# Queueing a group's output scaling behind the next fill's first two evacuations

## Chip, cores, metric

The kernel runs on one core of a Trainium2 chip. The metric is device time of one execution in microseconds (us). Times of single steps and instructions come from one profiled run of each kernel.

Engines are named as in the profile: PE (TensorE matmuls), PEld (its weight loads), DVE (VectorE), ACT (ScalarE), POOL (GpSimd).

## The reference

For each of 4 batches, 32 inducing rows attend to 12480 tokens, the tokens then attend to the 32 results, and every token goes through a two-layer network with a per-channel leaky ReLU.

```python
h   = mab(inducing, x)            # 32 x 128 per batch: softmax attention over 12480 tokens
y   = mab(x, h)                   # 12480 x 128: softmax attention over 32 rows
hid = y @ w_in                    # 128 -> 2048
g   = maximum(hid, 0) + alpha * minimum(hid, 0)
out = g @ w_out                   # 2048 -> 128
```

The leaky ReLU is split as `alpha*hid + (1-alpha)*relu(hid)`. So the output is a sum of two parts: a ReLU part through all 2048 channels, and a *linear term*, which is one small 128x128 product. Both are computed on unnormalised attention weights, and the output is divided by the softmax denominator at the very end. That division is the *output scaling*.

## The kernel before

The tokens are cut in groups of 512, 25 groups to a batch. A group takes four *steps*, j = 0 to 3. One step is a fill (four matmuls into four PSUM banks), four evacuations with ReLU by ACT or DVE, and one step later 16 output matmuls into an accumulator.

The kernel uses eight banks of PSUM, the memory that its matmuls write. Six form a ring for the fills and for side work. The two others are accumulators that groups use in turn.

```python
def fill(st, g, j):
    # four matmuls into the next four banks of the ring (K=32, 512 columns each)
    for r in range(4):
        mm(bank(), hW[32*r:32*r+32, j, :], rep[32*r:32*r+32, :w])     # cut
    if j == 2:
        linear(st, lin_groups(st.b, g))
    for r, (ps, i) in enumerate(banks):
        # a small clock model picks the engine that would be done first
        if ta <= td: nc.scalar.activation(out=gt[:, r, :w], in_=ps, func=RELU)
        else:        nc.vector.tensor_relu(gt[:, r, :w], ps)

def mm2(st, g, j, gt, done):
    acc = accs[(st.b * NG + g) % 2]
    # 16 matmuls: acc += gt.T @ W1                                      # cut
    if j == NJ - 1 and st.b * NG + g > 0:
        finish(st, g)          # DVE: ob = acc * 1/denominator, then the store

def lin_groups(b, g):          # even g: for g and for g + 1
    ...
def linear(st, groups):
    for k in range(NB):
        for r, g in enumerate(groups):
            mm(accs[(st.b*NG + g) % 2][:pp, k, :], rep..., hA...,
               start=(r == 1 and k == 0))   # starts the accumulator of g + 1

# main loop: the output matmuls of a step stand behind the fill of the next
for b, g, j in fills:
    gt, done = fill(states[b], g, j)
    for fn in tasks.pop((b * NG + g, j), []): fn()
    if prev is not None: mm2(*prev)
    prev = (states[b], g, j, gt, done)
```

The ring is short. Four banks of a fill plus four of the next are eight, but there are six, so a fill's third and fourth banks are the first and second banks of the fill before. Those two must be evacuated within one step.

The scaling of group g-1 is emitted after the evacuations of fill (g, 0), so DVE meets it at about fill (g, 1). The linear term in (g, 2), g even, starts the accumulator of group g+1, which is the one that group g-1 has just used, so it must wait until that scaling has read it.

`a_scores` and `a_accum` work on the next batch and stood in j=1, of odd and of even groups. `b_scores` and `b_den` stand in j=3 of even groups. Each takes one bank of the ring and some PE time.

The softmax here doesn't subtract the row's maximum and nothing guards it: scores larger than these inputs give would overflow.

Of the kernel before, what the change touches and what calls it, by code (L numbers as in the profile page):

```python
# [15 lines left out]
P = 128  # L16
# [8 lines left out]
def kernel(  # L25
# [64 lines left out]
    clk = {"P": 0.0, "A": 0.0, "D": 0.0}  # L90
    free = [0.0] * RING

    def bank():
        i = ring_n[0] % RING
        ring_n[0] += 1
        clk["P"] = max(clk["P"], free[i])
        return ring[i]

    def spent(e, ns, release=True):
        clk[e] = max(clk[e], clk["P"] + 100) + ns  # L100
        if release:
            free[(ring_n[0] - 1) % RING] = clk[e] + 100

    def mm(o, lhsT, rhs, start=True, stop=True, **kw):
        return pin(nc.tensor.matmul(o, lhsT, rhs, start=start, stop=stop, **kw))  # L105
# [163 lines left out]
    def h_sum(st):  # L269
        st.et = work.tile([P, 1], f32, name="et", tag="et")  # L270
        pin(nc.vector.reduce_sum(out=st.et[:], in_=st.es[:], axis=AXX))

    def h_den(st):
        ps = bank()
        mm(ps[:, 0:1], fold[:], st.et[:])
        rh = work.tile([P, 1], f32, name="rh", tag="rh")
        pin(nc.vector.reciprocal(out=rh[:], in_=ps[:, 0:1]))
        st.fr = work.tile([P, P], f32, name="fr", tag="fr")
        pin(nc.vector.tensor_scalar_mul(out=st.fr[:], in0=fold[:], scalar1=rh[:]))


    def h_transpose(st):
        ps = bank()
        mm(ps[:, :P], st.hacc[:], st.fr[:])
        st.hT4 = work.tile([C, P], bf16, name="hT4", tag="hT4")
        pin(nc.vector.tensor_copy(out=st.hT4[:], in_=ps[:, :P]))
        st.hT = st.hT4[:, 0:M]

    def h_weights(st):
        ps = bank()  # L290
        for r in range(4):
            mm(
                ps[32 * r : 32 * r + 32, :], st.hT,
                w_in_b[:, r * NJ * P : (r + 1) * NJ * P],
            )
        st.hW = work.tile([P, NJ, P], bf16, name="hW", tag="hW")
        pin(nc.vector.tensor_copy(out=st.hW[:].rearrange("m j k -> m (j k)"), in_=ps[:]))

    def h_linear(st):
        pa = bank()  # L300
        mm(pa[:, :C], st.hT4[:], Amat[:])
        st.hA = work.tile([P, C], bf16, name="hA", tag="hA")
        pin(nc.vector.tensor_copy(out=st.hA[:], in_=pa[:, :C]))
# [52 lines left out]
    def b_den(st, s):  # L356
        e2 = st.e2.pop(s)
        ps = bank()
        clk["P"] += 240
        spent("D", 250)  # L360
        if s < NS:
            for j in range(NB):
                mm(ps[:, j * NQ : (j + 1) * NQ], e2[:, j * P : (j + 1) * P], pick[:])
            rd = work.tile([P, NB, NQ], f32, name="rd", tag="rd")
            pin(nc.vector.reciprocal(
                out=rd[:].rearrange("p j q -> p (j q)"), in_=ps[:, : NB * NQ]
            ))
        else:
            for j in range(JR):
                mm(ps[:PR, j : j + 1], e2[:, j * PR : (j + 1) * PR], pick[0:M, 0:1])  # L370
            rd = work.tile([PR, JR, 1], f32, name="rdr", tag="rdr")
            pin(nc.vector.reciprocal(
                out=rd[:].rearrange("p j q -> p (j q)"), in_=ps[:PR, :JR]
            ))
        st.rden[s] = rd


    def shape_of(g):
        return (P, NB) if g < NS * NQ else (PR, JR)

    def fill(st, g, j):
        pp, nb = shape_of(g)
        w = pp * nb
        rep = st.rep[g]
        gt = gt_pool.tile([P, 4, GRP], bf16, name="gt", tag="gt")
        banks = []
        for r in range(4):
            ps = bank()
            mm(
                ps[:, :w], st.hW[32 * r : 32 * r + 32, j, :], rep[32 * r : 32 * r + 32, :w]  # L390
            )
            banks.append((ps, (ring_n[0] - 1) % RING))
        if j == 2:
            linear(st, lin_groups(st.b, g))
        ca, cd = w * 0.75 + 96, w * 1.04 + 68
        ready = clk["P"] + 150 + w * 0.42
        clk["P"] = ready - 50 + (240 if j == 2 and lin_groups(st.b, g) else 0)
        done = ready
        for r, (ps, i) in enumerate(banks):
            ta, td = max(clk["A"], ready) + ca, max(clk["D"], ready) + cd  # L400
            if ta <= td:
                clk["A"] = free[i] = ta
                pin(nc.scalar.activation(out=gt[:, r, :w], in_=ps[:, :w], func=RELU))  # L403
            else:
                clk["D"] = free[i] = td
                pin(nc.vector.tensor_relu(gt[:, r, :w], ps[:, :w]))  # L406
            free[i] += 150
            done = max(done, free[i])
        return gt, done

    def mm2(st, g, j, gt, done):
        pp, nb = shape_of(g)
        acc = accs[(st.b * NG + g) % 2]
        clk["P"] = max(clk["P"], done) + 4 * nb * 57
        begun = g % 2 == 1 and st.b + g > 1
        for r in range(4):
            c = r * NJ + j
            for k in range(nb):
                mm(
                    acc[:pp, k, :], gt[:, r, k * pp : (k + 1) * pp], W1[:, c, :],  # L420
                    start=(j == 0 and r == 0 and k == 0 and not begun), stop=False,
                    skip_group_check=True,
                )
        if j == NJ - 1 and st.b * NG + g > 0:
            finish(st, g)



# [1 line left out]
    def lin_groups(b, g):  # L430
        if g % 2 == 0 and (b, g) != (0, 0):
            return [g, g + 1] if g + 1 < NS * NQ else [g]
        return []
# [13 lines left out]
    def finish(st, g):  # L447
        pp, nb = shape_of(g)
        acc = accs[(st.b * NG + g) % 2]
        s, q = divmod(g, NQ)  # L450
        rd = st.rden[s]
        rq = rd[:, :, q : q + 1]
        rbc = bass.AP(tensor=rq.tensor, offset=rq.offset, ap=[rq.ap[0], rq.ap[1], [0, C]])
        ob = ob_pool.tile([P, NB, C], f32, name="ob", tag="ob")
        pin(nc.vector.tensor_tensor(  # L455
            out=ob[:pp, :nb, :], in0=acc[:pp, :nb, :], in1=rbc, op=MULT
        ))
        spent("D", nb * C * 1.04 + 68, release=False)
        t0 = st.b * N + g * GRP
        last_one = (st.b, g) == (B - 1, NG - 1)  # L460
        pin((nc.sync if last_one else nc.gpsimd).dma_start(  # L461
            out=out[t0 : t0 + pp * nb, :].rearrange("(p j) c -> p j c", j=nb),
            in_=ob[:pp, :nb, :],
        ))
        st.rep.pop(g)
# [4 lines left out]
    st = new_batch(0)  # L470
# [90 lines left out]
    n = len(order)  # L561
# [27 lines left out]
    states = {0: st}  # L589
    tasks = {}  # L590

    def at(slot, fn, j=1):
        tasks.setdefault((slot, j), []).append(fn)
# [15 lines left out]
    for b in range(B):  # L609
        base = b * NG  # L610
        for s in range(1, NS + 1):
            g = base + s * NQ - 4
            at(g, lambda b=b, s=s: b_scores(states[b], s), 3)
            at(g + 1, lambda b=b, s=s: b_rep(states[b], s), 3)
            at(g + 2, lambda b=b, s=s: b_den(states[b], s), 3)
        if b + 1 < B:
            n = b + 1

            def begin(n=n):
                states[n] = new_batch(n)  # L620

            at(base, begin)
            for i, u in enumerate(order):
                k = base + i * (NG - 13) // NS
                at(k, lambda n=n, u=u: a_load(states[n], u))
                at(k + 3, lambda n=n, u=u: a_xpose(states[n], u))
                at(k + 5, lambda n=n, u=u: a_scores(states[n], u))
                at(k + 8, lambda n=n, u=u: a_accum(states[n], u))
            k = base + NG - 5
            at(k, lambda n=n: h_sum(states[n]))  # L630
            at(k, lambda n=n: h_den(states[n]), 3)
            at(k + 1, lambda n=n: h_transpose(states[n]))
            at(k + 1, lambda n=n: h_weights(states[n]), 3)
            at(k + 2, lambda n=n: b_scores(states[n], 0))
            at(k + 2, lambda n=n: h_linear(states[n]), 3)
            at(k + 3, lambda n=n: b_rep(states[n], 0), 0)
            at(k + 3, lambda n=n: b_den(states[n], 0))

    prev = None
    for b, g, j in fills:  # L640
        gt, done = fill(states[b], g, j)
        for fn in tasks.pop((b * NG + g, j), []):
            fn()
        if prev is not None:
            mm2(*prev)
        prev = (states[b], g, j, gt, done)
    mm2(*prev)
    assert not tasks, tasks


# [28 lines left out]
```

## Time and profile before

| | before |
|---|---|
| median time | 617.5 us |
| PE busy | 97% of the span |
| DVE busy, ACT busy | 85%, 81% |
| a step in which nothing waits | 1.326 us (400 steps in all) |

These are the page's busy times, and its chain of work that ended last by engine:

```profile
span 615.2 us, 21846 instructions
...
PE 598.9 (97%) x9180; PEld 436.7 (71%) x9180; DVE 524.2 (85%) x935; ACT 500.8 (81%) x994; POOL 89.0 (14%) x151
...
PE 95%; DVE 0%; ACT 0%; issue 0%
```

PE looks full, but that is not the whole truth. In these records a fill matmul lasts 0.38 us and an output matmul 0.22 us, while output matmuls start every 0.056 us and those of a fill within 0.01 us of each other. So a wait of up to 0.3 us disappears under the tail of the matmul before it. The list of waits of PE: its entries are all start-up waits. The only one on the evacuation of a fill is this, and it too is of the first fills (at 30.55 us):

```profile
PE ring_81 L105 <- ACT gt L403: 0.4, 1, 0.4
```

I therefore read *start-to-start* times: a step's length is the time from its first fill matmul to the next step's. Its excess over the shortest step of the same make-up (the same tasks in it) seen in any of the profiles is its stall. The steps before group 2 of the first batch and the last step are left out. Summed by parity of g and by j, in us, the kernel before has:

| slot | even j=0 | even j=1 | even j=2 | even j=3 | odd j=0 | odd j=1 | odd j=2 | odd j=3 | sum |
|---|---|---|---|---|---|---|---|---|---|
| before | 0.1 | 1.5 | 1.8 | 1.8 | 4.5 | 0.4 | 5.9 | 2.9 | 18.8 |

By this measure about 19 of 617 us were waits. The start-up (the first 43 us) is not counted, and a wait that even the shortest step contains would not show. Here is a stall in the timeline, in steps (g, 1) and (g, 2) of an even group. The columns are start, length, engine, line, operation, output and inputs:

```profile
346.50 0.38 PE L105 MATMUL ring_82<-rep,hW 32*128 32x512 bf16 x1
346.51 0.39 PE L105 MATMUL ring_83<-rep,hW 32*128 32x512 bf16 x1
...
346.90 0.68 DVE L455 TENSOR_TENSOR ob<-acc_88,rd 128x512 f32<-128x512 f32 x1
346.98 0.60 ACT L403 ACTIVATE gt<-ring_82 128x512 bf16<-128x512 f32 x1 [0.24 <-ACT gt L403]
347.47 0.59 ACT L403 ACTIVATE gt<-ring_83 128x512 bf16<-128x512 f32 x1
347.50 0.68 DVE L406 TENSOR_SCALAR gt<-ring_84 128x512 bf16<-128x512 f32 x1
347.83 0.10 PEld L105 LDWEIGHTS <-hW 32*128 32x128 bf16 x4
...
347.84 0.38 PE L105 MATMUL ring_82<-rep,hW 32*128 32x512 bf16 x1
...
348.11 0.37 PE L105 MATMUL ring_83<-rep,hW 32*128 32x512 bf16 x1
...
348.12 0.22 PE L105 MATMUL acc_88<-hA,rep 32*128 32x128 bf16 x1
```

The scaling (`ob<-acc_88`) takes DVE at 0.39 us after the fill. ACT then has to evacuate both ring_82 and ring_83, and is done with the second at 348.06. The next fill's last matmul needs ring_83 and starts at 348.11 instead of 347.84. The linear term (`hA`) follows at once. The PE entry carries no idle time, although 0.27 us were lost between two matmuls. In this slot little of it counts: without the wait the linear term would have started 0.23 us after the fill anyway, so the step takes 1.613 us where the shortest of its make-up takes 1.542. In odd groups there is no linear term at j=2, and almost all of such a wait counts (1.583 us against 1.326).

### The profile page before, as it was taken

The page shows a single profiled execution, that of the slowest core. Times are in us where ns is not written, and L with a number is a line of the kernel's source. Part 1 is how long each engine was busy: PE and PEld are TensorE (multiplying, and loading weights), DVE is VectorE, ACT ScalarE, POOL GpSimd, SP SyncE. Part 2 cuts the span into 40 slices and gives each one's busy share as a digit, 9 for nine tenths or more (in the row PEclk, how much of TensorE's full clock was granted, in tenths as well). Part 3 has the DMA queues.
Part 4 walks back from the last instruction along what each step waited for, and adds up shares of the span by engine and source line. Part 5 has one row for each costly group of instructions (what it writes and reads, how often), then busy time and mean ns, then how long its engine had stood idle before and what let it go on. Part 6 is the DMA issues. An engine that isn't in the chain of part 4 may idle for free.

```text
span 615.2 us, 21846 instructions
## 1 busy us (share of the span) xinstructions
PE 598.9 (97%) x9180; PEld 436.7 (71%) x9180; DVE 524.2 (85%) x935; ACT 500.8 (81%) x994; POOL 89.0 (14%) x151
## 2 busy tenths in 40 slices
PE   5799999999999999999999999999999999999996
PEld 4577777777777777777777777777777777777774
DVE  4688888889988888888988888888898888888885
ACT  2678888888888888888878888888888888888884
POOL 7241112101011111111011112110101011011010
PEclk9999999999999999999999999999999999999999
DMA  9824879652125598763122588864121221221211
GB/s 141 173 69 99 185 154 180 152 113 86 51 84 129 125 177 184 144 151 87 58 96 91 111 169 168 171 154 122 62 81 54 86 95 53 80 96 46 87 56 43
DMA packets 87458, 68.66 MB, mean 112 GB/s; under 512 B 53200, under 2 KB 80736, under 8 KB 87360
## 3 DMA queue, kind: packets, MB, share of 16 engines
q0 software_dynamic: 21456, 39.82, 26.2%
q1 hardware_dynamic: 65904, 27.45, 20.4%
q8 instruction: 72, 1.18, 0.8%
q14 instruction: 26, 0.21, 0.1%
HBM read 39.94 MB, written 28.62 MB: 111 GB/s over the span
## 4 chain that ended last, share of the span: by engine, by line
PE 95%; DVE 0%; ACT 0%; issue 0%
PE acc_87 L105 32%; PE acc_88 L105 32%; PE ring_82 L105 5%; PE ring_86 L105 5%; PE ring_84 L105 5%; PE ring_83 L105 5%; PE ring_81 L105 5%; PE ring_85 L105 5%; DVE gt L406 0%; ACT rep L342 0%; ACT gt L403 0%; PE ring_83 L543 0%; PE ring_81 L543 0%; DVE e1T L194 0%; DVE ob L455 0%
## 5 line engine op out<-in xcount | busy, mean ns | idle before, releaser
L105 PEld LDWEIGHTS <-gt 128*128 128x128 bf16 x6272 | 352.9, 98 | 83.0 <-issue 73.6
L105 PE MATMUL acc_87<-W_169,gt 128*128 128x128 bf16 (+1 forms) x3136 | 209.8, 220 | 0.0
L105 PE MATMUL acc_88<-W_169,gt 128*128 128x128 bf16 (+1 forms) x3136 | 209.6, 220 | 0.0
L461 POOL DMA_DIRECT2D out_dram<-ob x99 | 53.6, 541 | 501.6 <-DVE ob L455 482.2
L403 ACT ACTIVATE gt<-ring_86 128x512 bf16<-128x512 f32 (+1 forms) x159 | 92.2, 580 | 17.3 <-ACT gt L403 9.8
L403 ACT ACTIVATE gt<-ring_82 128x512 bf16<-128x512 f32 (+1 forms) x164 | 95.6, 583 | 12.2 <-ACT gt L403 7.9
L403 ACT ACTIVATE gt<-ring_84 128x512 bf16<-128x512 f32 (+1 forms) x151 | 88.5, 586 | 20.0 <-ACT gt L403 15.0
L105 PE MATMUL ring_84<-rep,hW 32*128 32x512 bf16 (+1 forms) x273 | 103.5, 379 | 0.0
L105 PE MATMUL ring_83<-rep,hW 32*128 32x512 bf16 (+1 forms) x273 | 103.0, 377 | 0.0
L105 PE MATMUL ring_81<-rep,hW 32*128 32x512 bf16 (+1 forms) x270 | 102.0, 378 | 0.7 <-ACT gt L403 0.4
L406 DVE TENSOR_SCALAR gt<-ring_81 128x512 bf16<-128x512 f32 (+1 forms) x139 | 91.3, 657 | 13.2 <-PE ring_83 L105 4.8
L105 PE MATMUL ring_86<-rep,hW 32*128 32x512 bf16 (+1 forms) x269 | 101.4, 377 | 0.1
L403 ACT ACTIVATE gt<-ring_85 128x512 bf16<-128x512 f32 x149 | 89.3, 599 | 12.3 <-ACT gt L403 8.4
L105 PE MATMUL ring_82<-rep,hW 32*128 32x512 bf16 (+1 forms) x258 | 97.4, 378 | 0.0
L105 PE MATMUL ring_85<-rep,hW 32*128 32x512 bf16 (+1 forms) x257 | 97.2, 378 | 0.0
L406 DVE TENSOR_SCALAR gt<-ring_83 128x512 bf16<-128x512 f32 (+1 forms) x128 | 84.3, 659 | 12.9 <-PE ring_85 L105 6.0
L406 DVE TENSOR_SCALAR gt<-ring_84 128x512 bf16<-128x512 f32 x122 | 83.6, 685 | 13.5 <-PE ring_86 L105 5.3
L403 ACT ACTIVATE gt<-ring_83 128x512 bf16<-128x512 f32 (+1 forms) x145 | 86.8, 598 | 10.3 <-ACT gt L403 7.5
L403 ACT ACTIVATE gt<-ring_81 128x512 bf16<-128x512 f32 x131 | 78.9, 602 | 19.4 <-ACT gt L403 13.0
L406 DVE TENSOR_SCALAR gt<-ring_85 128x512 bf16<-128x512 f32 (+1 forms) x108 | 72.1, 667 | 12.5 <-issue 5.4
L406 DVE TENSOR_SCALAR gt<-ring_86 128x512 bf16<-128x512 f32 x110 | 75.2, 684 | 7.4 <-ACT gt L403 3.0
L406 DVE TENSOR_SCALAR gt<-ring_82 128x512 bf16<-128x512 f32 x94 | 64.5, 687 | 10.1 <-issue 3.4
(299 smaller groups left out, 377.9 us busy)
## 6 DMA issues: line engine op xcount, KB each, us to landing
out_dram<-ob POOLq DMA_DIRECT2D x96, 256.0 KB, 2.6
rep<-e2d SPq DMA_DIRECT2D x92, 128.0 KB, 3.3
xn<-in_x_dram POOLq DMA_DIRECT2D x18, 512.0 KB, 6.0
xn<-in_x_dram POOLq DMA_DIRECT2D x12, 256.0 KB, 7.7
w_out_f<-in_moe_w_out_dram POOLq DMA_DIRECT2D x1, 1024.0 KB, 13.5
w_in_b<-in_moe_w_in_dram POOLq DMA_DIRECT2D x1, 512.0 KB, 11.4
xT<-xn SPq DMA_TRANSPOSE x18, 4.7
out_dram<-ob POOLq DMA_DIRECT2D x3, 96.0 KB, 2.0
```

What stands on the lines that cost most here:

```text
L105: return pin(nc.tensor.matmul(o, lhsT, rhs, start=start, stop=stop, **kw))
L403: pin(nc.scalar.activation(out=gt[:, r, :w], in_=ps[:, :w], func=RELU))
L406: pin(nc.vector.tensor_relu(gt[:, r, :w], ps[:, :w]))
L461: pin((nc.sync if last_one else nc.gpsimd).dma_start(out=out[t0 : t0 + pp * nb, :].rearrange("(p j) c -> p j c", j=nb), in_=ob[:pp, :nb, :],))
```

## The change

The change evacuates the two banks that the next fill needs first, and scales the finished group after that. The clock model, which picks ACT or DVE for each evacuation, gets other latencies, and two side tasks leave j=1. The core of the diff:

```diff
@@ fill
-        ready = clk["P"] + 150 + w * 0.42
-        clk["P"] = ready - 50 + (240 if j == 2 and lin_groups(st.b, g) else 0)
+        ready = clk["P"] + 240 + w * 0.42
+        clk["P"] = ready - 135 + (240 if j == 2 and lin_groups(st.b, g) else 0)
         for r, (ps, i) in enumerate(banks):
+            if r == 2:
+                while held:
+                    finish(*held.pop())
@@ mm2
-        clk["P"] = max(clk["P"], done) + 4 * nb * 57
+        t = clk["P"]
+        for r in range(4):
+            t = max(t, done[r]) + nb * 57
+        clk["P"] = t + 85
         if j == NJ - 1 and st.b * NG + g > 0:
-            finish(st, g)
+            held.append((st, g))
@@ tasks of the next batch
-                at(k + 5, lambda n=n, u=u: a_scores(states[n], u))
-                at(k + 8, lambda n=n, u=u: a_accum(states[n], u))
+                at(k + 5, lambda n=n, u=u: a_scores(states[n], u), 0)
+                at(k + 8, lambda n=n, u=u: a_accum(states[n], u), 2)
 # cut: held = [] and a list of done times in fill; clock-model lines in h_den, h_transpose, h_weights, h_linear, b_den;
 # one last finish() after the loop
```

More of the change, by code (lines that the diff above doesn't have):

```diff
@@ L274, in h_den @@
         ps = bank()
+        clk["P"] += 250
+        spent("D", 500)
         mm(ps[:, 0:1], fold[:], st.et[:])
@@ L283, in h_transpose @@
         ps = bank()
+        clk["P"] += 300
+        spent("D", 250)
         mm(ps[:, :P], st.hacc[:], st.fr[:])
@@ L290, in h_weights @@
         ps = bank()
+        clk["P"] += 320
+        spent("D", 600)
         for r in range(4):
@@ L300, in h_linear @@
         pa = bank()
+        clk["P"] += 80
+        spent("D", 250)
         mm(pa[:, :C], st.hT4[:], Amat[:])
@@ L358, in b_den @@
         ps = bank()
-        clk["P"] += 240
+        clk["P"] += 130
         spent("D", 250)
@@ L379, in shape_of @@
         return (P, NB) if g < NS * NQ else (PR, JR)
+    held = []
     def fill(st, g, j):
@@ L395, in fill @@
         ca, cd = w * 0.75 + 96, w * 1.04 + 68
-        ready = clk["P"] + 150 + w * 0.42
-        clk["P"] = ready - 50 + (240 if j == 2 and lin_groups(st.b, g) else 0)
-        done = ready
+        ready = clk["P"] + 240 + w * 0.42
+        clk["P"] = ready - 135 + (240 if j == 2 and lin_groups(st.b, g) else 0)
+        done = []
         for r, (ps, i) in enumerate(banks):
+            if r == 2:
+                while held:
+                    finish(*held.pop())
             ta, td = max(clk["A"], ready) + ca, max(clk["D"], ready) + cd
@@ L407, in fill @@
             free[i] += 150
-            done = max(done, free[i])
+            done.append(free[i])
         return gt, done
@@ L647 @@
     mm2(*prev)
+    finish(*held.pop())
     assert not tasks, tasks
```

## The prediction

> **What bounds the kernel now.** TensorE (PE): busy 97% in the page's engine table, 95% of the chain that ended last. The Trainium skill ("Trainium Kernel Development and Optimization", Performance Expectations) warns that matmul busy time is a poor metric because matmuls are pipelined; this trace agrees, for stalls hide inside it. So I read start-to-start times in the timeline. A step (4 fill matmuls, 16 output matmuls) takes 1.326 us when nothing waits. Fill to first output matmul is always 0.317 us, output to next fill always 0.152 us: neither ever waits. What waits are the later fill matmuls, for a bank. Summing each kind of step over its shortest example (g = group, j = step of it) gives: odd g j=2 5.9 us, odd g j=3 2.9, odd g j=0 4.4, even g j=2 1.3, the rest about 1. So about 15 of 617 us can be recovered at all.
>
> **Mechanism before.** VectorE (DVE) scales the finished group (0.68 us) from 0.39 to 1.07 us after the fill of j=1 starts, ahead of its evacuation. ACT then evacuates the first two banks one after the other, the second ends at 1.56, and the next fill (at 1.326) gets its last bank 0.27 us late.
>
> **What changes.** The instruction order shows the same matmuls and evacuation counts (DVE 701, ACT 899), none added. In 98 of 100 groups the j=1 fill is now evacuated ACT, DVE, ACT, ACT, and the scaling sits behind that DVE evacuation. a_scores moves from j=1 to j=0 (0.33 us of PE, no net change), a_accum from j=1 to j=2 (0.34 us, likewise).
>
> Gain: the first two banks come free at 1.07 and 1.20 us, before 1.326, so the j=2 stall goes, and with a_scores out of j=1 the odd j=3 stall too: 5.9 + 2.9 + 1.3 = 10 us. The 0.16 us stall in odd j=0 follows b_den (a third bank freed at 1.56+0.05, next fill at 1.43) and stays: b_den and its evacuation order don't change.
>
> Loss: in even groups, the linear term in j=2 starts the accumulator of group g+1, the one that group g-1 just used. In the changed program its second matmul waits for exactly that scaling. Unhindered it starts 0.23 us after the j=2 fill, that is 1.555 us after the j=1 fill. The scaling now runs: DVE evacuation starts 0.514, the next DVE instruction 0.608 later = 1.12, ends 1.80, plus 0.054 until PE starts (seen where fills waited for DVE) = 1.857. So 0.30 us new wait. The matmuls behind it wait too: the Trainium skill ("TensorE: Matmul & The Clock Gate", Part 3, The mechanism) has matmuls in strict FIFO; the trace's matmuls start in program order. 47 such steps x 0.30 = 14 us.
>
> Net, an estimate from these durations: 617.5 - 10 + 14 = 621 us.
>
> **Prediction: 621 us, 613 to 626 (8 in 10). Faster by over 2%: 0.04; within 2%: 0.93; slower by over 2%: 0.03.**
>
> **What would show each step.** (1) Odd j=2 and j=3 steps near 1.33 us. (2) Odd j=0 after b_den still about 1.48. (3) Even j=2 steps: before 1.54 to 1.61, after about 1.85 (plus 0.34 where a_accum now follows). In the list of waits PE should wait on the linear matmuls for the DVE scaling. (4) DVE scaling starting 1.12 us after the fill instead of 0.39. (5) Busy times of ACT and DVE unchanged, TensorE clock unchanged.
>
> **What would make it wrong.** If DVE reached the scaling earlier than 1.12 us, or the linear term started later (other waits before it), the loss shrinks and the gain stands: about 608. If three ACT evacuations in a row, or a_accum's bank directly behind the linear term, delay banks of j=2 or j=3, some of the 10 us stay and it nears 628.

## The result

| | before | changed |
|---|---|---|
| median time (6 runs each) | 617.51 us | 621.16 us |
| ratio changed / before | | 1.0058 (95%: 1.0045 to 1.0071) |

A ratio here is the mean time of one kernel's fast runs over that of the other's in the same rounds, so it is not quite the ratio of the two medians. The change costs 0.6%. The outputs are correct.

The page after, in the same lines:

```profile
span 619.1 us, 21674 instructions
...
PE 598.9 (97%) x9179; PEld 434.5 (70%) x9180; DVE 531.0 (86%) x935; ACT 500.7 (81%) x994; POOL 89.0 (14%) x151
```

PE's busy time is 598.9 us in both, while the span grew by 3.9 us. Busy time cannot tell this story. The timeline of the same two steps of the same group can:

```profile
348.69 0.38 PE L105 MATMUL ring_82<-rep,hW 32*128 32x512 bf16 x1
...
349.16 0.60 ACT L417 ACTIVATE gt<-ring_82 128x512 bf16<-128x512 f32 x1 [0.24 <-ACT gt L417]
349.21 0.69 DVE L420 TENSOR_SCALAR gt<-ring_83 128x512 bf16<-128x512 f32 x1
349.66 0.59 ACT L417 ACTIVATE gt<-ring_84 128x512 bf16<-128x512 f32 x1
349.81 0.68 DVE L472 TENSOR_TENSOR ob<-acc_88,rd 128x512 f32<-128x512 f32 x1
350.01 0.10 PEld L105 LDWEIGHTS <-hW 32*128 32x128 bf16 x4
350.02 0.38 PE L105 MATMUL ring_86<-rep,hW 32*128 32x512 bf16 x1
...
350.03 0.39 PE L105 MATMUL ring_83<-rep,hW 32*128 32x512 bf16 x1
...
350.25 0.21 PE L105 MATMUL acc_87<-hA,rep 32*128 32x128 bf16 x1
...
350.55 0.21 PE L105 MATMUL acc_88<-hA,rep 32*128 32x128 bf16 x1
...
350.56 0.23 PE L105 MATMUL acc_87<-hA,rep 32*128 32x128 bf16 x1
```

The first aim is reached: ring_83 is evacuated by DVE at once, and the fill's fourth matmul starts at 350.03, not 0.27 us late. But the scaling of acc_88 now starts 1.12 us after the fill and ends at 350.49. The linear term's first matmul, into acc_87, starts at 350.25. Its second goes into acc_88 and does not start before 350.55. Every matmul behind it waits too. The step takes 1.840 us, where 1.542 us is the shortest of its make-up.

The groups of instructions show the linear matmuls (output, inputs, count, then busy us, mean ns and idle us before them), first in the kernel before and then in the changed one:

```profile
L105 PE MATMUL acc_88<-hA,rep 32*128 32x128 bf16 (+1 forms) x196 | 19.1, 215 | 0.0
```

```profile
L105 PE MATMUL acc_88<-hA,rep 32*128 32x128 bf16 (+1 forms) x196 | 22.4, 215 | 1.7
```

The mean matmul is as long as ever. Only 1.7 us of the wait count as idle time before these, and 1.9 before those of the other accumulator (acc_87), since the tail of the first linear matmul (it ends 0.09 us before the second starts) covers most of it. PE's list of waits does not name the scaling at all.

The stall table is the measure that does not miss it (us):

| slot | even j=0 | even j=1 | even j=2 | even j=3 | odd j=0 | odd j=1 | odd j=2 | odd j=3 | sum |
|---|---|---|---|---|---|---|---|---|---|
| before | 0.1 | 1.5 | 1.8 | 1.8 | 4.5 | 0.4 | 5.9 | 2.9 | 18.8 |
| changed | 0.6 | 1.4 | 11.8 | 1.3 | 4.9 | 0.5 | 1.0 | 0.1 | 21.6 |

The bank stalls of odd groups (j=2 and j=3) fell by 7.7 us and even j=2 grew by 10.0. With 0.4 us more in the other slots the sum of stalls rose by 2.7 us. Of the 3.9 us of span, the sum of the shortest steps adds 0.4, the time from the last store's issue to the end of the span adds 1.0 (5.4 before, 6.4 after), and the start-up was 0.2 us shorter.

### The profile page after: what moved, and what is told of

Read it like the earlier page. It is cut to its first block, busy times and chain, and to the rows that moved or that the text cites. A ratio compares the mean times of both kernels' runs of the same rounds, so it can differ in the third digit from the quotient of the medians.

```text
span 619.1 us, 21674 instructions
## 1 busy us (share of the span) xinstructions
PE 598.9 (97%) x9179; PEld 434.5 (70%) x9180; DVE 531.0 (86%) x935; ACT 500.7 (81%) x994; POOL 89.0 (14%) x151
## 4 chain that ended last, share of the span: by engine, by line
PE 74%; DVE 1%; issue 0%; DVEq 0%
PE acc_87 L105 26%; PE acc_88 L105 26%; PE ring_84 L105 4%; PE ring_82 L105 4%; PE ring_86 L105 4%; PE ring_83 L105 4%; PE ring_81 L105 3%; PE ring_85 L105 3%; DVE ob L472 0%; DVE gt L420 0%; DVEq L420 0%
## 5 line engine op out<-in xcount | busy, mean ns | idle before, releaser
L417 ACT ACTIVATE gt<-ring_84 128x512 bf16<-128x512 f32 (+1 forms) x163 | 95.8, 588 | 22.9 <-ACT gt L417 19.1
L417 ACT ACTIVATE gt<-ring_81 128x512 bf16<-128x512 f32 (+1 forms) x153 | 91.3, 597 | 18.6 <-ACT gt L417 14.1
L417 ACT ACTIVATE gt<-ring_86 128x512 bf16<-128x512 f32 (+1 forms) x159 | 92.2, 580 | 17.0 <-ACT gt L417 12.6
L417 ACT ACTIVATE gt<-ring_82 128x512 bf16<-128x512 f32 (+1 forms) x154 | 89.6, 582 | 13.7 <-ACT gt L417 9.4
L417 ACT ACTIVATE gt<-ring_83 128x512 bf16<-128x512 f32 x138 | 82.7, 599 | 9.6 <-ACT gt L417 5.5
L417 ACT ACTIVATE gt<-ring_85 128x512 bf16<-128x512 f32 x132 | 79.2, 600 | 13.0 <-ACT gt L417 7.3
```

The costliest lines, as they stand in the source:

```text
L417: pin(nc.scalar.activation(out=gt[:, r, :w], in_=ps[:, :w], func=RELU))
```

## The experiments

My theory: the queued scaling removes the bank stalls, but the linear term waits for it through the shared accumulator, and that costs more than the bank stalls did. The rivals were that a_accum stands badly behind the linear term, that three ACT evacuations in a row hold up the ring, that the task moves are what costs time, or that the clock model is.

Each run was timed in 3 rounds against the kernel before on the same chip, and all gave correct outputs. The kernel before took 617.16 us (median) with e1 to e4, and 617.11 us with e5 to e8. All edits are to the changed kernel unless said otherwise.

Stalls by slot in all runs, in us, for the slots that move:

| run | even j=2 | odd j=0 | odd j=2 | odd j=3 | sum of all slots | time | ratio to before |
|---|---|---|---|---|---|---|---|
| before | 1.8 | 4.5 | 5.9 | 2.9 | 18.8 | 617.1 to 617.5 | 1 |
| changed | 11.8 | 4.9 | 1.0 | 0.1 | 21.6 | 621.16 | 1.0058 |
| e1_parity | 3.0 | 5.1 | 0.6 | 0.1 | 12.6 | 611.12 | 0.9902 |
| e2_lin3 | 0.3 | 0.7 | 1.0 | 0.1 | 6.0 | 605.31 | 0.9809 |
| e3_hold_nomove | 5.7 | 4.6 | 1.0 | 3.1 | 18.3 | 617.05 | 1.0012 |
| e4_move_nohold | 3.0 | 4.7 | 7.9 | 0.1 | 19.5 | 618.33 | 1.0018 |
| e5_clock_only | 2.1 | 4.3 | 5.9 | 2.7 | 19.3 | 617.85 | 1.0013 |
| e6_hold_all4 | 39.5 | 4.6 | 0.6 | 12.0 | 60.2 | 659.84 | 1.0691 |
| e7_before_lin3 | 7.0 | 0.6 | 6.0 | 2.8 | 19.8 | 618.03 | 1.0014 |
| e8_lin3_nomove | 0.2 | 0.5 | 1.0 | 3.2 | 8.9 | 608.13 | 0.9851 |

### e1_parity: scale early only where the linear term waits

```diff
         if j == NJ - 1 and st.b * NG + g > 0:
-            held.append((st, g))
+            if g % 2 == 1 or g == NG - 1:
+                finish(st, g)
+            else:
+                held.append((st, g))
# cut: after the loop, all that is still held is finished
```

> The changed kernel, but the scaling of odd groups (whose accumulator the next linear term reuses) goes back ahead of the evacuations; only even groups' scaling stays queued behind two evacuations. Theory (the loss is the linear term waiting for the scaling): even j=2 steps without a_accum fall from 1.84 to 1.61 us (the bank stall of before comes back, 0.07 us net), odd j=2 and j=3 stay at 1.33; total 621.2 - 47 x 0.226 = about 610.5 us, faster than both kernels. Rival (the loss is a_accum and the linear term in one slot, or three ACT evacuations in a row): even j=2 stays near 1.84 and the total near 621.

Measured: 611.12 us. Even j=2 steps without a_accum took 1.613 us and odd j=2 and j=3 stayed near 1.33. The task slots and a_accum behind the linear term are those of the changed kernel, so neither is the loss. The theory held. The order of ACT and DVE in the evacuations is not that of the changed kernel (replaying the clock model, it differs in 94 of 400 steps), so e1 leaves three ACT evacuations in a row open; e2 settles them. The timeline of the same step shows the linear term close behind the fill again, all eight matmuls in one row:

```profile
346.29 0.65 PE L105 MATMUL ring<-rep,hW 32*128 32x512 bf16 x4
...
346.58 0.40 PE L105 MATMUL acc<-hA,rep 32*128 32x128 bf16 x8
```

### e2_lin3: let the linear term come one step later

```diff
-        if j == 2:
+        if j == 3:
             linear(st, lin_groups(st.b, g))
-        ... (240 if j == 2 and lin_groups(st.b, g) else 0)
+        ... (240 if j == 3 and lin_groups(st.b, g) else 0)
```

> The changed kernel with the linear term moved from j=2 to j=3 of even groups, so that it comes one step later than the scaling that it waits for. Theory: no wait for the scaling is left (47 x 0.30 = 14 us), and as the linear term now also lengthens the b_den step by 0.21 us, the 0.16 us bank stall after b_den (24 times) goes too: even j=2 steps 1.33 us without a_accum, odd j=0 after b_den 1.33; total 621.2 - 14.0 - 3.7 = about 603.5 us. Rival (three ACT evacuations or a_accum's bank at fault): even j=2 keeps an excess of about 0.3 us over 1.33 (or 0.3 over 1.66 with a_accum), total 617 to 621.

Measured: 605.31 us, ratio 0.9809 (95%: 0.9793 to 0.9825), the fastest of all. The ACT and DVE order of the evacuations is that of the changed kernel in every step (by a replay of the clock model), so three ACT evacuations in a row are cleared as well. The timeline of the same group (this profile does not number banks):

```profile
342.15 0.68 DVE L472 TENSOR_TENSOR ob<-acc,rd 128x512 f32<-128x512 f32 x1
342.34 0.10 PEld L105 LDWEIGHTS <-hW 32*128 32x128 bf16 x4
342.35 0.39 PE L105 MATMUL ring<-rep,hW 32*128 32x512 bf16 x4
...
342.68 1.07 PE L105 MATMUL acc<-W,gt 128*128 128x128 bf16 x16
...
343.68 0.39 PE L105 MATMUL ring<-rep,hW 32*128 32x512 bf16 x4
...
343.90 0.38 PE L105 MATMUL acc<-hA,rep 32*128 32x128 bf16 x8
```

The scaling stands as late as in the changed kernel (1.13 us after its fill at 341.02), but it ends at 342.83, over 1 us before the linear term. All eight linear matmuls run as one row at 343.90. The j=2 step is a bare 1.326 us.

The stall after b_den went too. In the kernel before, 19 of 20 odd j=0 steps after a full b_den step took 1.48 us; as I read it, because b_den is short and takes a bank. In e2 the linear term lengthens that step, and the same steps are at their shortest (1.33 us, or 1.66 us with a_scores in them). Summed over the 24 steps after b_den, the stall fell from 4.2 to 0.4 us, which is 3.8 us of the gain.

### e3_hold_nomove: queued scaling, tasks back in j=1

```diff
-    a_scores(states[n], u), 0)   /   a_accum(states[n], u), 2)
+    a_scores(states[n], u))      /   a_accum(states[n], u))
```

> The changed kernel with a_scores and a_accum back in j=1 (scaling still behind two evacuations). Theory: where a_accum stands in the even j=1 step (18 to 21 of 47) the linear term comes 0.34 us later and finds the scaling done, so those j=2 steps take 1.54 us and only the others 1.84: 6.3 us less than the changed kernel; the 0.16 us stall of odd j=3 after a_scores returns (18 times, 2.9 us): about 618 us. Rival (moving the tasks is what cost time): the whole loss goes, about 607 to 608 us.

Measured: 617.05 us (three runs within 0.2 us, a fourth at 620.8 with a clock of 0.99). In the 18 steps after a j=1 step that holds a full a_accum, the linear term no longer waits, and even j=2 fell from 11.8 to 5.7 us. The odd j=3 stall came back with 3.1 us. So the two parts of the change work against each other: moving a_accum out of j=1 removed the delay that had let the linear term find the scaling done. The rival's 607 us is excluded.

### e4_move_nohold: scaling back in front, tasks moved

```diff
-            held.append((st, g))
+            finish(st, g)
# cut: no finish() is left to do after the loop
```

> The changed kernel with the scaling back ahead of the evacuations (clock model and task moves kept). Theory: no PE wait on the linear term (even j=2 1.61 us), but the odd j=2 stall is back and larger, 0.27 us where ACT evacuates the first two banks, 0.41 us where DVE has the second one behind the scaling: about 626 us. Rival (queueing the scaling is what cost time on the whole): faster than before, 608 to 612 us.

Measured: 618.33 us, which neither the theory (about 626) nor the rival (608 to 612) had. It is slower than the kernel before, as expected, but by 0.2% (95%: 0.03% to 0.33%) where I expected 1.4%; and it is faster than the changed kernel (621.16), where I expected it slower. Even j=2 is 1.61 us as said. Odd j=2 steps in groups with a_scores in j=0, where DVE has the second bank behind the scaling, took 1.42 us, so the stall was 0.10 us, not 0.41. The timeline of the j=1 step of such a group shows why:

```profile
400.61 0.40 PE L105 MATMUL ring<-rep,hW 32*128 32x512 bf16 x4
400.72 0.69 DVE L472 TENSOR_TENSOR ob<-acc,rd 128x512 f32<-128x512 f32 x1
...
401.32 0.68 DVE L420 TENSOR_SCALAR gt<-ring 128x512 bf16<-128x512 f32 x1
...
401.93 0.10 PEld L105 LDWEIGHTS <-hW 32*128 32x128 bf16 x4
```

The scaling starts 0.11 us after the fill, not 0.39. I had taken 0.39 from the kernel before as if it were a property of the scaling. It is the time at which DVE came free, and an a_scores step, 0.33 us longer, gives DVE that much more time.

### e5_clock_only: the clock model alone

The changed kernel with the edits of e3 and e4 both.

> Only the clock model of the change: scaling ahead of the evacuations, tasks in their old slots. The evacuations go to nearly the same engines as in the kernel before. Theory (the clock model does nothing by itself): 616 to 619 us, the stalls by slot as in the kernel before (even j=2 1.8, odd j=2 5.9, odd j=3 2.9 us). Rival (it moves the time by itself): outside 614 to 621 us.

Measured: 617.85 us, ratio 1.0013 (95%: 0.9998 to 1.0028). The stalls by slot are those of before. With scaling and tasks in their old places, the clock model does nothing that this can see.

### e6_hold_all4: the dose doubled

```diff
-            if r == 2:
-                while held:
-                    finish(*held.pop())
     # ... all four evacuations ...
+        while held:
+            finish(*held.pop())
         return gt, done
```

> The dose doubled: the changed kernel with the scaling behind all four evacuations of the j=1 fill (two of them on DVE, so one more DVE instruction of 0.61 us ahead of it). Theory (the linear term waits for the scaling, one for one with its place on DVE): the 40 even j=2 steps that wait grow from 1.84 to 2.45 us (2.78 with a_accum), that is 24 us. The odd j=2 fill is then evacuated behind the scaling again, ACT taking its first two banks, and odd j=3 (or j=2) shows a stall of about 0.28 us (47 times, 13 us): total about 645 to 660 us. Rival (the loss comes from a_accum's bank or three ACT evacuations in a row, which this run does not have in the j=1 fill): even j=2 steps do not grow, total at or below 621 us.

Measured: 659.84 us. Even j=2 steps took 2.437 us, and 2.774 us with a_accum. One more DVE evacuation (0.61 us from start to start) ahead of the scaling made them 0.597 us longer than in the changed kernel, nearly one for one. The wait is now long enough to come out from under the matmul tails. These are the timeline of the same group and the list of waits of PE (engine and line, what it waited for, us in total, times, longest):

```profile
371.02 0.40 PE L105 MATMUL ring<-rep,hW 32*128 32x512 bf16 x4
...
371.25 0.21 PE L105 MATMUL acc<-hA,rep 32*128 32x128 bf16 x1
371.42 0.68 DVE L470 TENSOR_TENSOR ob<-acc,rd 128x512 f32<-128x512 f32 x1
...
372.15 0.38 PE L105 MATMUL acc<-hA,rep 32*128 32x128 bf16 x7 [0.69 <-DVE ob L470]
```

```profile
PE acc L105 <- DVE ob L470: 30.0, 47, 0.7
```

In this run the profile itself names the culprit: 47 waits on the scaling. The other 12 us, in odd j=3, came as expected from ACT evacuating the two urgent banks behind one another after the late scaling.

### e7_before_lin3: only the linear term moved, in the kernel before

The edit of e2, made to the kernel before.

> The kernel before with only the linear term moved from j=2 to j=3. Asks whether that move helps without the queued scaling. Theory: no. The 0.27 us bank stall in even j=2, which the linear term's own start hid all but 0.07 us of, comes into the open (about 20 times 0.2 and 27 times 0.05 us, 5 us more), and the b_den stall of odd j=0 goes (24 x 0.155 = 3.7 us less): about 619 us, within 0.5% of the kernel before. Rival (the linear term's slot alone made the 605 us): 605 to 610 us.

Measured: 618.03 us. Even j=2 stalls rose to 7.0 us and the stall after b_den went (odd j=0 from 4.5 to 0.6 us). The ratio's interval (0.9999 to 1.0029) includes no change. Without the queued scaling, moving the linear term only lays open a bank stall that it had covered. The gain of e2 is of the pair.

### e8_lin3_nomove: e2 without the task moves

The edits of e2 and e3 both.

> The fastest version so far (linear term in j=3, scaling behind two evacuations) with a_scores and a_accum back in j=1. Theory: the task moves are worth only the 0.16 us stall of odd j=3 after a_scores (18 to 20 times, 3 us): about 608.5 us. Rival (the moves carry much of the gain): 611 us or more.

Measured: 608.13 us. Odd j=3 shows the 3.2 us again. Of the 12 us that e2 gains on the kernel before, the moves carry about 3.

## Why the prediction was right

The predicted 621 us stood against 621.16 measured. Point by point:

1. *Odd j=2 and j=3 near 1.33 us*: right. Their stalls fell from 5.9 and 2.9 to 1.0 and 0.1 us, which is 7.7 us where I had summed 8.8.
2. *The stall after b_den stays*: right, 4.5 before and 4.9 us after in odd j=0. That it goes when the linear term shares the slot was not in the prediction, and e2 shows it.
3. *Even j=2 about 1.85 us*: right, 1.840 us, and 2.178 us with a_accum. The count was wrong. I took 47 such steps, but only 40 wait. The other 7 follow a j=1 step that is longer anyway (a task in it, or a stall at the start of a batch), so the linear term comes late enough. 40 times the 0.298 us of one wait is 11.9 us, not 14, and the table has 11.8.
4. *PE's list of waits should show the linear matmuls waiting for the scaling*: wrong. The wait of 0.30 us, of which 0.09 us lies outside a matmul's recorded length, is too short for that list. Only e6 brought it there.
5. *Scaling 1.12 us after the fill*: right to the digit (348.69 to 349.81).
6. *Busy times unchanged*: right for ACT (500.8, 500.7) and for the clock. DVE rose from 524.2 to 531.0 us with the same 935 instructions.

The terms of the sum were each a little too large. The gain in odd groups was 7.7 us, not 8.8. The net loss in even j=2 was 10.0 us (1.8 to 11.8), not 12.7 (14 less the 1.3 counted as gain). With 0.4 us more in the other slots the stalls rose by 2.7 us where I had about 4, and the match to 0.2 us owes something to chance: 0.4 us more came from the shortest steps and 1.0 us at the end of the span, after the last store is issued, which was not predicted. I do not know the cause of that last part. It varied between 5.4 and 6.4 us over the ten profiles, 5.4 to 5.9 where the scaling of the last full group was not held (e1 is one of these), 6.05 to 6.4 where it was; no run was made to settle it. The trace tells where most of it lies: the last store landed 1.80 us after its issue before and 2.53 us after, 0.7 of the 1.0 us. Why it landed later stays open. One reading in the prediction was loose, and nothing rests on it: in steps without side work, fill to first output took 0.301 to 0.318 us, not always 0.317.

What is shown, and by what: that the loss is the linear term's wait for the scaling is shown by e1 and e2 (take the wait away in two ways, and it goes) and by e6 (lengthen it, and the loss grows with it). That the clock model alone is innocent is shown by e5. The prediction leaned on matmuls being held in strict program order, as the Trainium skill ("TensorE: Matmul & The Clock Gate", Part 3, The mechanism) states. The trace agrees: in the changed kernel the third linear matmul, whose accumulator is free, starts at 350.56, just after the blocked second one at 350.55. Its weight load came only at 350.55 too, so the trace shows that the order was kept, and not which of the two held the third matmul.

## What to carry to other kernels

When an instruction is moved back in a queue to make way for urgent work, list everything that waits for *its* result, not only what waited behind it: here the buffer it frees was wanted 0.3 us before the new time. If a consumer is in the way, move the consumer one slot too. Queueing the scaling cost 0.6% as it was made, moving the linear term alone gained nothing (0.1% more time, within the noise), and both together took 1.9% off (1.5% with the side tasks left in j=1).

On an engine whose records overlap, measure waits as start-to-start times against the shortest step of the same kind. Busy shares and lists of waits missed a loss of 11.8 us in 40 pieces of about 0.3 us. Only when the pieces were 0.9 us did both show it (e6, where PE busy fell to 93%).

## What the Trainium skill lacked or had wrong

- "Trainium Kernel Development and Optimization", Performance Expectations, says that matmul busy time is a bad metric for how close a kernel is to roofline and weight-load busy time a good one. The first half is borne out: 97% PE in kernels of 605, 617 and 621 us. The second is too coarse for stalls of this size: PEld was busy 72%, 71% and 70% of the span in these three, because its total (434.5 to 436.7 us) hardly moves. Start-to-start times are not offered as a measure there, and they found the stalls.
- "TensorE: Matmul & The Clock Gate", Back-to-back issue gap, gives about 81 ns per matmul as the sustained rate of weight load and matmul pairs at N=128. In runs of 16 such pairs here, matmuls started every 56 ns, which that section gives as the gap of an isolated matmul; longer runs do not occur here.
- "TensorEngine Tiling (Array Packing)", Key Properties, says that switching the tiling mode drains the engine, without a figure. Here the first output matmul started 0.317 us after the last fill matmul (N=512, four row tiles), and the next fill 0.152 us after the last output matmul, in full steps that did not wait. The gaps between like matmuls that "TensorE: Matmul & The Clock Gate", Wait — 56ns, not 53.3ns?, gives are 0.216 us (N=512) and 0.056 us (N=128); the second is seen here, the first in no run. The difference, about 0.2 us a step or 80 us over 400 steps as an estimate from both, is more than all the stalls of any kernel here (60.2 us at most). That it is the drain is not shown; no run tested it.
- No page that I found gives the time from the end of a DVE or ACT instruction to the start of a matmul that waits for it. Here it was 0.05 us: a bank's evacuation that ended at 348.06 released a fill at 348.11, and a scaling that ended at 350.49 a linear matmul at 350.55.
